# Gated linear attention and two expert layers on one core: ScalarE's order in the first two expert steps is taken from the program

## The chip, the core and the metric

The kernel runs on one core of a Trainium2 chip. The metric is the device time of one execution in microseconds (us), as the median of several runs. Beside it there is one profiled execution, from which the trace comes. TensorE is PE in the profile (its weight loads are PEld), VectorE is DVE, ScalarE is ACT, GpSimd is POOL and SyncE, which issues most transfers, is SP.

## The reference, cut to what matters

```python
state = f[t, :, None] * state + outer(k[t], v[t])        # f = sigmoid(f_logit), per head
y[t]  = q[t] @ state                                     # 4 x 8 heads, 768 tokens, width 48
x     = y laid out as (3072 tokens, 384)
x     = square(relu(x @ w_in)) @ w_out                   # 384 -> 2048 -> 384
logits = x @ w_gate                                      # 8 experts
e      = argmax(logits, axis=1)                          # one expert for each token
out[n] = softmax(logits)[n, e[n]] * (relu(x[n] @ w1[e[n]]) @ w2[e[n]])   # 384 -> 1024 -> 384
```

All of it is float32. Products that need full precision are made of three matmuls: each operand is split into a rounded part (`hi`) and the rest (`lo`), and the sum takes lo with hi, hi with lo and hi with hi.

## The kernel before

The first part walks through eight groups of 384 tokens. For each group it makes the attention output, then the first expert layer in 16 slices i (`moe_h` gives `ph`, `moe_act` gives `gg`, `gh` and `gl`, `moe_out` adds into `po`), and then the routing of its tokens (`route`). TensorE, ScalarE, VectorE and GpSimd run in the written order there. `moe_out` of a slice is issued two slices after its `moe_h`, so the last two slices of the last group have their `moe_out` back to back at its end.

The second part has expert steps. A step of kind D takes 256 tokens of one expert through that expert's two matrices in 8 slices: `step_h` (9 matmuls into `ph`, then `hh` on ScalarE and `hl` on VectorE) and, two slices later, `step_out` (6 matmuls into `qo`). The weights of one step come in eight pieces j (`load_w`, SyncE's queue, 384 KB each) into `raw`; each piece is then split (`split_w`, `split_part`): ScalarE makes `w_hi`, and VectorE or GpSimd makes `w_lo` (for step 1, GpSimd has the odd j, by `lo_pool`). A piece of `raw` can be loaded again when both have read it. Two sets of `w_hi` and `w_lo` alternate: step 0 and step 2 use set 0, step 1 uses set 1, which held the second matrix of the first layer until the last group's `moe_out`.

Step 0's pieces are split in the last group. Step 1's pieces are issued in the program's text in step 0, by `split_plan`, in the order j = 0, 1, 4, 2, 5, 3, 6, 7, each behind one slice's `step_h`. Also in step 0, `final_tables` runs piecewise through `hook`: it finishes the routing of the last group (`route`: logits `pl`, the one-hot `oh`, the counts `pc`, the rows `abr`, the table `pslot`) and computes which expert and which tokens the steps from 2 on take (down to `esi` for the weights and `sel`, `pi`, `ids` for the tokens). This is a chain of some eighty small VectorE instructions with four stops on TensorE (`pl`, `pc`, `pslot`, `pi`), whose places among TensorE's matmuls are fixed.

What sets the order: a scheduler in the compiler orders the instructions of each engine by its own estimate of when they can run, and may move them far from their place in the text. For engines named in `manual_schedule` the order is the program's. In the first two steps this is TensorE only, in the later ones TensorE and ScalarE. VectorE, GpSimd and SyncE are ordered by the scheduler in all steps.

Of the kernel before, what the change touches and what calls it, by code (L numbers as in the profile page):

```python
# [56 lines left out]
def gla_moe_moe_kernel(ctx: ExitStack, tc: tile.TileContext, qk, ft, vt, w_in, w_out, w_gate, w_gateT, w_e, q, k, v, f_logit, out, dbg=None):  # L57
# [969 lines left out]
    def run_steps(s0, s1, hook=None, pend=(), flush=True):  # L1027
        pend = list(pend)
        for s in range(s0, s1):
            if s == NALWAYS - 1:  # L1030
                tc.mark_branch_hint_location("rest")
            for i in range(8):
                pend.append((s, i, *step_h(s, i)))
                while len(pend) > (2 if KINDS[s] == "D" else 3):
                    step_out(*pend.pop(0))
                if i == 0 and s + 2 != NEARLY:
                    load_x(s + 2)
                if KINDS[s] == "S" and i % 2:
                    load_w(s + 1, i // 2)
                for t, j in SPLITS.get((s, i), ()):  # L1040
                    split_w(t, j)
                    if t + 1 != NEARLY or early["ready"]:
                        load_w(t + 1, j)
                if hook:
                    hook(s, i)
                if i == (5 if KINDS[s] == "D" else 3):
                    prep_next(s + 1)
        if flush:
            for p in pend:
                step_out(*p)  # L1050
        return pend
# [3 lines left out]
        if s < NEARLY:  # L1055
            next(fin, None)

    with tc.manual_schedule(engines={mybir.EngineType.PE}):
        left = run_steps(0, NEARLY, hook, flush=False)
    with tc.manual_schedule(engines={mybir.EngineType.PE, mybir.EngineType.Activation}):  # L1060
        run_steps(NEARLY, NALWAYS, pend=left)
# [291 lines left out]
```

## Time and profile before

| | |
|---|---|
| median of 3 runs | 834.55 us (834.1 to 838.1) |
| the profiled execution's own time | 835.33 us |
| its span, first to last instruction | 833.6 us |
| TensorE busy | 797.7 us, 96% of the span |
| VectorE busy | 554.3 us, 66% |
| ScalarE busy | 412.6 us, 49% |
| GpSimd busy | 160.0 us, 19% |
| granted TensorE clock, mean | 0.99 |

The span lies 1.7 us below the own time, and the own time 0.8 us above the median. In the trace the last group runs from 496.6 to 558.5 us, step 0 from 558.5 to 579.8, step 1 to 598.8.

### The profile page before, as it was taken

How to read it: one execution, taken by the hardware profiler on the slowest of the kernel's cores; microseconds unless marked ns; L12 is line 12 of the kernel's file. 1: busy time of each engine (PE TensorE's matmuls, PEld its weight loads, DVE VectorE, ACT ScalarE, POOL GpSimd, SP SyncE). 2: the span in 40 equal slices, each digit the busy share in tenths (PEclk: the TensorE clock that was granted, in tenths of full speed). 3: DMA queues.
4: the chain of work that ended last, by engine and by line, in shares of the span. 5: the costliest groups of instructions: out<-in, count | busy, mean ns of one | idle time of the engine just before them, and what ended most of it. 6: DMA issues, size and time to landing. Idle time of an engine off the chain costs nothing.

```text
span 833.6 us, 14582 instructions
## 1 busy us (share of the span) xinstructions
PE 797.7 (96%) x5343; PEld 747.8 (90%) x5343; DVE 554.3 (66%) x1266; ACT 412.6 (49%) x814; POOL 160.0 (19%) x154
## 2 busy tenths in 40 slices
PE   5799999999999999999999999989999899999995
PEld 4566669999999999999999999989999899898995
DVE  7988769867767757857757844558467555556641
ACT  2233366454455455455454454662565565556551
POOL 2000000000000000000000002021666556555651
PEclk9999999999999999999999999999999999999998
DMA  9786410121130121131130015322866676868640
GB/s 245 215 247 200 128 38 22 41 76 41 40 95 22 41 76 41 40 84 34 40 77 1 1 37 190 105 77 83 292 214 194 229 256 204 270 194 270 194 150 28
DMA packets 40687, 100.61 MB, mean 121 GB/s; under 512 B 5662, under 2 KB 12642, under 8 KB 40480
## 3 DMA queue, kind: packets, MB, share of 16 engines
q1 hardware_dynamic: 37024, 90.14, 36.0%
q0 software_dynamic: 3584, 9.46, 3.0%
q8 instruction: 44, 0.72, 0.4%
q14 instruction: 35, 0.29, 0.1%
HBM read 89.73 MB, written 10.24 MB: 120 GB/s over the span
## 4 chain that ended last, share of the span: by engine, by line
PE 76%; DVE 7%; DMA 6%; issue 5%; ACT 4%; POOL 0%; SPq 0%; POOLq 0%; DVEq 0%; ACTq 0%
PE po L421 21%; PE ph L391 20%; PE qo L984 8%; PE ph L964 8%; DVE w_lo L596 4%; DMA raw<-w_e 4%; PE pa L271 3%; PE py L310 3%; PE ph L381 3%; PE py L301 2%; ACT w_hi L595 2%; PE pu L295 2%; PE ph L952 2%; DMA xT<-xT 2%; PE pk L264 1%
## 5 line engine op out<-in xcount | busy, mean ns | idle before, releaser
L397 ACT ACTIVATE gg<-ph 128x384 f32<-128x384 f32 x128 | 62.7, 490 | 177.2 <-PE ph L391 121.8
L404 DVE TENSOR_TENSOR gl<-gg,gh 128x384 fp32r<-128x384 f32 x112 | 63.4, 566 | 92.8 <-ACT gh L402 91.5
L391 PE MATMUL ph<-xh,w_lo 128*128 128x384 f32 x336 | 119.0, 354 | 1.0 <-ACT gg L397 1.0
L421 PE MATMUL po<-w_hi,gl 128*128 128x384 f32 x336 | 113.5, 338 | 2.3 <-DVE gl L404 2.3
L391 PE MATMUL ph<-xl,w_hi 128*128 128x384 f32 x336 | 114.8, 342 | 0.6 <-DVE xl L168 0.6
L391 PE MATMUL ph<-xh,w_hi 128*128 128x384 f32 x336 | 114.3, 340 | 0.0
L421 PE MATMUL po<-w_hi,gh 128*128 128x384 f32 x336 | 113.3, 337 | 0.0
L421 PE MATMUL po<-w_lo,gh 128*128 128x384 f32 x336 | 112.9, 336 | 0.0
L596 DVE TENSOR_TENSOR w_lo<-raw,w_hi 128x768 fp32r<-128x768 f32 x63 | 94.3, 1499 | 24.9 <-ACT w_hi L595 19.8
L596 POOL TENSOR_TENSOR w_lo<-raw,w_hi 128x768 fp32r<-128x768 f32 x49 | 90.7, 1868 | 83.7 <-ACT w_hi L595 81.4
L595 ACT ACTIVATE w_hi<-raw 128x768 fp32r<-128x768 f32 x112 | 93.8, 839 | 21.8 <-DMA raw<-w_e 20.5
L969 DVE SCALAR_TENSOR_TENSOR hl<-ph,hh 128x256 fp32r<-128x256 f32 (+1 forms) x128 | 48.8, 386 | 77.7 <-ACT hh L968 73.5
L691 POOL MEMSET xg<- 128x385 f32 x4 | 2.1, 556 | 479.3 <-PE py L301 479.3
L968 ACT ACTIVATE hh<-ph 128x256 fp32r<-128x256 f32 (+1 forms) x128 | 45.2, 356 | 96.0 <-PE ph L964 75.7
L964 PE MATMUL ph<-xh,w_lo 128*128 128x256 f32 x288 | 82.7, 287 | 5.9 <-DVE w_lo L596 5.9
L445 DVE SCALAR_TENSOR_TENSOR junk<-rows,wgb 128x384 f32<-128x384 f32 x144 | 79.8, 554 | 3.3
L964 PE MATMUL ph<-xl,w_hi 128*128 128x256 f32 x288 | 81.2, 282 | 0.0
L964 PE MATMUL ph<-xh,w_hi 128*128 128x256 f32 x288 | 81.0, 281 | 0.0
L391 PEld LDWEIGHTS ph<-xh,w_lo 128*128 128x128 f32 x336 | 63.1, 188 | 7.3 <-issue 3.3
L398 ACT ACTIVATE gg<-gg 128x384 f32<-128x384 f32 x128 | 67.2, 525 | 4.0
L984 PE MATMUL qo<-w_hi,hl 128*128 128x384 f32 x192 | 66.4, 346 | 1.9 <-DVE hl L969 1.2
L421 PEld LDWEIGHTS po<-w_hi,gl 128*128 128x128 f32 x336 | 63.1, 188 | 2.9 <-DVE gl L404 2.7
(226 smaller groups left out, 1682.0 us busy)
## 6 DMA issues: line engine op xcount, KB each, us to landing
raw<-w_e SPq DMA_DIRECT2D x128, 384.0 KB
qk<-qk SPq DMA_DIRECT2D x46, 192.0 KB
stg<-w_in SPq DMA_DIRECT2D x8, 768.0 KB
stg<-w_out SPq DMA_DIRECT2D x8, 768.0 KB
f<-ft SPq DMA_DIRECT2D x24, 226.2 KB
xs<-rows SPq DMA_DIRECT2D x8, 577.5 KB
v<-vt SPq DMA_DIRECT2D x24, 192.0 KB
wgb<-w_gateT SPq DMA_DIRECT2D x1, 1536.0 KB
```

What stands on the lines that cost most here:

```text
L391: nc.tensor.matmul(ph, lhsT=w[:, sl], rhs=x[:, k, :], start=(n == 0), stop=(n == 8))
L397: nc.scalar.activation(out=gg, in_=ph, func=AF.Relu)
L398: nc.scalar.activation(out=gg, in_=gg, func=AF.Square)
L404: nc.vector.tensor_tensor(out=gl, in0=gg, in1=gh.bitcast(F32), op=ALU.subtract)
L421: nc.tensor.matmul(po[m], lhsT=a[:, sl], rhs=w[:, ws], start=(i == 0 and n == 0), stop=(i == NF - 1 and n == len(terms) - 1),)
L445: nc.vector.scalar_tensor_tensor(out=junk, in0=rows[:, m, 0:DM], scalar=1.0, in1=wgb[0][:, e, :], op0=ALU.mult, op1=ALU.mult, accum_out=lg ...
L595: nc.scalar.activation(out=hi, in_=src, func=AF.Copy)
L596: eng.tensor_tensor(out=lo, in0=src, in1=hi.bitcast(F32), op=ALU.subtract)
L964: nc.tensor.matmul(ph, lhsT=wslice(s, w, (i * 3 + k) * 128, 128), rhs=x[:, k, :], start=(n == 0), stop=(n == 8))
L968: nc.scalar.activation(out=hh, in_=ph, func=AF.Relu)
L969: nc.vector.scalar_tensor_tensor(out=hl, in0=ph, scalar=0.0, in1=hh.bitcast(F32), op0=ALU.max, op1=ALU.subtract)
L984: nc.tensor.matmul(out_t[s][m], lhsT=x[:, sl], rhs=wslice(s, w, 3 * F2 + i * DM, DM), start=(i == 0 and n == 0), stop=(i == 7 and n == 2),)
```

## The change

ScalarE is added to the engines whose order is the program's in steps 0 and 1.

```diff
-    with tc.manual_schedule(engines={mybir.EngineType.PE}):
+    with tc.manual_schedule(engines={mybir.EngineType.PE, mybir.EngineType.Activation}):
         left = run_steps(0, NEARLY, hook, flush=False)
```

No instruction is added or taken away; TensorE's order is the same. ScalarE's order changes, and with it the scheduler's orders for VectorE, GpSimd and SyncE. In the rows below `raw_5027` to `raw_5034` are the pieces j = 0 to 7, `w_hi_150` is set 0 and `w_hi_151` set 1, and `hh<-ph_5698`, `5730`, `5767`, `5820`, `5842` belong to the slices 0 to 4 of step 0.

ScalarE at the end of the last group and the start of step 0, before: the last three instructions of the last group's last slice (L397, L398, L402) stand behind a split of step 1's piece 5.

```order
L595 ACTIVATE w_hi_151<-raw_5032 128x768
L397 ACTIVATE gg<-ph 128x384
L398 ACTIVATE gg<-gg 128x384
L402 ACTIVATE gh<-gg 128x384
L595 ACTIVATE w_hi_150<-raw_5033 128x768
L595 ACTIVATE w_hi_150<-raw_5034 128x768
L438 ACTIVATE rows<-po_5171 128x384
L438 ACTIVATE rows<-po_5173 128x384
L595 ACTIVATE w_hi_151<-raw_5033 128x768
L968 ACTIVATE hh<-ph_5698 128x256
```

The same place in the changed kernel:

```order
L397 ACTIVATE gg<-ph 128x384
L398 ACTIVATE gg<-gg 128x384
L402 ACTIVATE gh<-gg 128x384
L595 ACTIVATE w_hi_150<-raw_5033 128x768
L595 ACTIVATE w_hi_150<-raw_5034 128x768
L438 ACTIVATE rows<-po_5171 128x384
L438 ACTIVATE rows<-po_5173 128x384
L968 ACTIVATE hh<-ph_5698 128x256
L595 ACTIVATE w_hi_151<-raw_5027 128x768
L463 ACTIVATE xt_5044<-pt 128x384
L968 ACTIVATE hh<-ph_5730 128x256
L595 ACTIVATE w_hi_151<-raw_5028 128x768
```

All eight splits of step 1, six of which stood in the last group, now stand in step 0, one behind each `hh`. Step 2's first six splits (`w_hi_150` of the pieces 0, 1, 4, 2, 5, 3), which stood between the second and the fourth `hh` of step 1, stand one behind each `hh` from step 1's third on.

VectorE between `oh` and the counts `pc` in step 0 (a piece of the difference; `sl` is the first instruction that reads `pc`, and om, ex and ss belong to the gate's value, which is off the way to `pslot`):

```order
 L479 SCALAR_TENSOR_TENSOR rk<-d,rev 128x24
 L481 TENSOR_REDUCE rm<-rk 128x3
-L535 TENSOR_SCALAR om<-ex 128x24
 L483 TENSOR_TENSOR oh<-rev,rm 128x24
-L536 RECIPROCAL om<-om 128x24
 L969 SCALAR_TENSOR_TENSOR hl<-ph_5767,hh 128x256
-L537 TENSOR_TENSOR ex<-ex,om 128x24
-L539 TENSOR_REDUCE ss<-ex 128x3
+L596 TENSOR_TENSOR w_lo<-raw_5031,w_hi_151 128x768
 L496 TENSOR_TENSOR sl<-pc,base 128x24
-L540 TENSOR_SCALAR ss<-ss 128x3
 L497 TENSOR_TENSOR base<-pc,base 128x8
```

A split of piece 4 now stands ahead of `sl`. A little further on, up to the rows `abr` from which `pslot` is made:

```order
+L596 TENSOR_TENSOR w_lo<-raw_5029,w_hi_151 128x768
 L639 TENSOR_REDUCE nb_5892<-gt_5890 128x8
 L504 TENSOR_SCALAR hl<-si 128x3
 L505 TENSOR_SCALAR hl<-si 128x3
-L969 SCALAR_TENSOR_TENSOR hl<-ph_5820,hh 128x256
+L969 SCALAR_TENSOR_TENSOR hl<-ph_5842,hh 128x256
 L825 TENSOR_TENSOR nb_5886<-nb_5886,nb_5892 128x8
 L507 CAST hf<-hl 128x6
 L826 TENSOR_TENSOR nb_5892<-nb_5892,taken 128x8
-L830 SCALAR_TENSOR_TENSOR co<-one_5052,nb_5886 128x8
+L535 TENSOR_SCALAR om<-ex 128x24
 L515 TENSOR_SCALAR abr_5046<-iblk,hf,tok_85 128x96
```

A split of piece 2 and the `hl` of slice 4 now stand ahead of `abr`, and so does `om`, which waits for ScalarE's `ex`. Further on a split of piece 6 stands between `pslot` and `sel`. On GpSimd the splits of the pieces 1, 5 and 3, three of which stood in the last group, now stand behind the tables' constants, ahead of that of piece 7 and of the gathers of step 2's tokens. On SyncE the loads of step 2 keep their places; those of step 3 now stand behind the reads of all later steps' expert numbers and of `tot`.

## Rows read from the trace of the kernel before

**Rows 1.** The waits of TensorE over the span: total us, times, longest us.
```profile
PE ph L964 <- DVE w_lo L596: 5.9, 3, 2.0
```
**Rows 2.** The chain that ended last, in order of time: start us, us, what.
```profile
505.60 1.57 PE po L421 x9
...
550.06 3.24 DMA raw<-w_e
...
562.00 1.06 PE ph L964 x9
```
**Rows 3.** The timeline of ScalarE at the last group's end: start us, us, idle before.
```profile
553.33 0.85 ACT L595 ACTIVATE w_hi<-raw 128x768 fp32r<-128x768 f32 x1 [2.04 <-DMA raw<-w_e]
554.08 0.47 ACT L397 ACTIVATE gg<-ph 128x384 f32<-128x384 f32 x1
```
**Rows 4.** The timeline of TensorE: earlier in the last group, and at its end.
```profile
507.01 1.14 PE L460 MATMUL pt<-ident,rows 128*128 128x128 f32 x9
507.91 0.42 PE L391 MATMUL ph<-xh,w_lo 128*128 128x384 f32 x1
...
553.87 0.34 PE L421 MATMUL po<-w_hi,gh 128*128 128x384 f32 x1
556.54 0.44 PE L421 MATMUL po<-w_hi,gl 128*128 128x384 f32 x1 [2.33 <-DVE gl L404]
...
561.75 0.36 PE L964 MATMUL ph<-xh,w_lo 128*128 128x256 f32 x1
```
**Rows 5.** Windows: stretch, length, busy us of PE, PEld, DVE, ACT, POOL; PEclk; DMA.
```profile
559.50:560.50 1.00, 1.00 (x7) 1.00 (x6) 0.00 (x0) 0.00 (x0) 0.00 (x0) 0.50 0.70 194
...
666.00:667.00 1.00, 1.00 (x10) 1.00 (x10) 0.59 (x1) 0.47 (x2) 0.00 (x0) 1.00 0.73 252
```
**Rows 6.** The timeline of TensorE in step 0: the stops of the tables.
```profile
567.03 0.18 PE L488 MATMUL pc<-oh,tri 128*128 128x8 bf16 x1
...
571.60 0.52 PE L530 MATMUL pslot<-abr 128*96 128x256 f32 x3
...
579.55 0.39 PE L655 MATMUL pi<-sel,slot 96*128 96x18 f32 x2 [0.39 <-DVE sel L651]
```
**Rows 7.** The timeline of VectorE in step 0.
```profile
567.45 0.18 DVE L496 TENSOR_TENSOR sl<-pc,base 128x24 f32<-128x24 f32 x1
...
570.79 0.32 DVE L515 TENSOR_SCALAR abr<-iblk,hf,tok 128x96 fp32r<-128x96 bf16 x1
571.03 0.35 DVE L523 TENSOR_SCALAR abr<-ipos,hf 128x256 fp32r<-128x256 bf16 x1
...
579.32 0.17 DVE L651 TENSOR_TENSOR sel<-wso,pp 96x18 fp32r<-96x18 f32 x1
```
**Rows 8.** A window over most of step 0.
```profile
562.00:580.00 18.00, 17.61 (x138) 17.08 (x138) 15.36 (x85) 4.84 (x12) 1.81 (x1) 1.00 0.10 35
```
**Rows 9.** The timeline of TensorE in step 1: first matmuls of four slices.
```profile
584.21 0.28 PE L964 MATMUL ph<-xh,w_lo 128*128 128x256 f32 x1
...
587.60 0.28 PE L964 MATMUL ph<-xh,w_lo 128*128 128x256 f32 x1
...
589.73 0.28 PE L964 MATMUL ph<-xh,w_lo 128*128 128x256 f32 x1
...
591.83 0.28 PE L964 MATMUL ph<-xh,w_lo 128*128 128x256 f32 x1
```
**Rows 10.** The timelines of VectorE and GpSimd where both split.
```profile
601.24 0.96 DVE L596 TENSOR_TENSOR w_lo<-raw,w_hi 128x768 fp32r<-128x768 f32 x1 [0.31 <-ACT w_hi L595]
...
605.60 4.82 DVE L596 TENSOR_TENSOR w_lo<-raw,w_hi 128x768 fp32r<-128x768 f32 x1 [0.31 <-ACT w_hi L595]
...
605.93 3.66 POOL L596 TENSOR_TENSOR w_lo<-raw,w_hi 128x768 fp32r<-128x768 f32 x2
...
533.29 1.85 POOL L596 TENSOR_TENSOR w_lo<-raw,w_hi 128x768 fp32r<-128x768 f32 x1 [22.66 <-ACT w_hi L595]
...
534.21 1.34 DVE L404 TENSOR_TENSOR gl<-gg,gh 128x384 fp32r<-128x384 f32 x1 [3.09 <-ACT gh L402]
```

## The prediction, made before the changed kernel ran

> **What bounds the kernel now.** I read the waits of TensorE first, then the chain that ended last, and then the timelines of the four engines around the places where it leaves TensorE. TensorE is busy for 96% of the span, so what counts is where it stands still. Between 505 and 600 us the chain goes off to the loads of `raw`: step 1's piece landing at 553.3 us ends a load of 3.24 us [rows 2]. ScalarE had waited 2.04 us for it, because a split of step 1's piece 5 stands in its order ahead of the last slice's `gg`, and `gg` starts only at 554.08 [rows 3]. TensorE's last `moe_out` needs `gl` and starts at 556.54, where the `po` before it began at 553.87: with the usual 0.17 between two starts 2.5 us are lost [rows 4]. Then the granted clock falls: it is 0.50 at 560 us, the lower of its two levels, 1.2 in place of 2.4 GHz [rows 5]. From 556.54 to the second `ph` of step 0 at 561.75 it takes 5.2 us; at full clock 9 `po` take 1.57, 9 `ph` 1.06 [rows 2] and the 9 transposes 0.90 (507.01 to 507.91) [rows 4], in all 3.53. So the fall cost 1.7. Three other waits of 2.0 us [rows 1] brought no fall (the clock is 1.00 behind the one that ended at 665.5 [rows 5]).
>
> Step 0 is bound otherwise. VectorE is busy 15.36 of the 18 us from 562 to 580, ScalarE 4.84 and GpSimd 1.81 [rows 8]: the tables keep VectorE nearly full. The last `abr` ends at 571.38 and TensorE takes `pslot` at 571.60 without a wait; for `pi` it waits 0.39 us for `sel` [rows 6, 7]. In step 1 a slice takes 2.10 us (589.73 to 591.83), but the one at 584.21 takes 3.39: 1.3 us are lost [rows 9], where ScalarE has step 2's splits ahead of the copies that free `qo`.
>
> **The change part by part.**
>
> *What it removes.* In the last group ScalarE waits for no piece of step 1 any more; step 0's pieces had landed before (their splits start without a wait for a transfer). `gg` of the last slice follows its `ph` as in the other slices, `gl` is ready by 553.4, and TensorE goes on at 554.04. That removes 2.5 of wait and 1.7 of clock. Everything in step 0 now lies 4.2 us earlier. The 1.3 of step 1 goes as well: two `hh` and both `qo` copies stand ahead of step 2's splits. The wait of 0.4 at `pi` is counted anew below, so it comes off too. Removed in all: 2.5 + 1.7 + 1.3 + 0.4 = 5.9 us.
>
> *What ScalarE takes up in step 0.* Eight splits of 0.85 [rows 3], 6.8 us, beside 4.84 of work in 18 [rows 8]. Each stands behind an `hh` and can hold up the next one by at most 0.85; `step_out` uses `hh` and `hl` two slices later, more than 2 us on. Cost nothing. If that cover were gone it would be up to 0.85 a slice.
>
> *What VectorE takes up.* Four splits, 0.96 each when VectorE is alone [rows 10], in an engine that is full. I walk the new order row by row with the durations of the trace, TensorE 4.2 us earlier (`pc` 562.9 in place of 567.03).
> First stop, `pslot`. `hh` of slice 2 ends at 562.4, ScalarE's split of piece 4 at 563.15, VectorE's at 564.1. Only then comes `sl`, for which `pc` was there at 563.3: 0.8 late. The split of piece 2 costs 0.9 a little later. `hl` of slice 4 must now pass ahead, and `om` waits 0.3 for `ex`, which on ScalarE stands behind the split of piece 5 and ends at 567.8. The six `abr` end at 569.55. TensorE has done its matmuls at 567.44 (571.60 less 4.16). It waits 2.1 us. In short: about 2.3 more on the way from `pc` to `abr`, less the 0.2 that this way had to spare [rows 6, 7].
> Second stop, `pi`. The way from `pslot` to `sel` gets the split of piece 6 (0.9) and the gate's small instructions, which were earlier before; the old wait of 0.4 becomes 1.4 if nothing else happens.
>
> *GpSimd beside VectorE.* This is the cost that the trace shows only for large instructions. At 605.60 VectorE starts a split and takes 4.82 us in place of 0.96; GpSimd works on two splits from 605.93 to 609.59 [rows 10]. VectorE stands still while GpSimd splits, though it had begun first. A `gl` of 384 elements takes 1.34 with GpSimd's split ending at 535.14 [rows 10]. Both read two tensors from SBUF, as many of the tables' instructions do. In the changed step 0 GpSimd splits four pieces, 1.85 each [rows 10], where it split one. Piece 1 falls beside the argmax, where TensorE has two slices of other work; piece 5 beside the six `abr`, which read one tensor and by the rows of other such instructions go on; piece 3 (572.4 to 574.25) beside the tables behind `pslot`, and piece 7 (577.3 to 579.2) beside VectorE's own split of piece 6, which starts at 576.9. The bounds are nothing, as for an instruction with one SBUF operand, and all of what is left of 1.85 at each collision. The nearest rows are held wholly, so I take that: 3.3 more at `pi`, 4.7 us in all.
>
> The Trainium skill (SBUF — State Buffer, section Who interferes with whom) says that a VectorE instruction with two SBUF inputs contends with a GpSimd instruction that reads SBUF, which the rows bear out. It also says that whichever issues first has the ports for the whole instruction; the row at 605.60 says otherwise, since VectorE was first by 0.33 us and lost. By the page the split of piece 6 would keep going; that is a rival below.
>
> *The clock.* A wait of 2.5 was followed by the fall, three of 2.0 were not. The wait at `pslot`, 2.1, lies between; that at `pi`, 4.7, lies above. I take one fall, 1.7; bounds none and two.
>
> *What moves at no cost.* Step 2's gathers of tokens start about 2 us later, but are read at 594; its loads keep their places in SyncE's queue and come 2 us later than before, while the first split that needs one moved back by more. The transfer of the last group's rows is issued some 4 us later and still ahead of those gathers. Step 3's loads, pushed behind the reads on SyncE, are split a step later, past 600 us. From there on the order is the old one and the whole tail only shifts.
>
> **Sum.** Added 2.1 + 4.7 + 1.7 = 8.5, removed 5.9: plus 2.6 us. On the profiled execution's own 835.33 that is 837.9; the median lies 0.8 below that execution, so the forecast is 837.1, 0.3% above 834.55. This is within 0.5% (4.2 us), about what a measurement of this kernel can tell from no change.
>
> **The rivals.**
>
> *Small instructions aren't held.* Then `pi` costs 1.4: 2.1 + 1.4 - 5.9 = -2.4 us, 832.2; with a fall of the clock after `pslot` -0.7, 833.8. For it: the tables' instructions are far shorter than those held in the rows, and no row has one beside a split. Against it: nothing in the held ones depends on their length. Chance 0.2.
>
> *Who starts first keeps the ports.* The split of piece 6 starts 0.4 ahead of GpSimd's piece 7 and isn't held, so `pi` costs 2.9: 2.1 + 2.9 + 1.7 - 5.9 = +0.8, 835.4. Against it speaks the 4.82. This is the rule of the Trainium skill's page SBUF — State Buffer. Chance 0.15.
>
> *Slower: `abr` is held too.* The six `abr` read one tensor, but the one with 256 columns takes 0.35 and the one with 96 takes 0.32 [rows 7]: 160 columns more for 0.03 us, where a split of 768 takes 0.96. So it runs in a faster way, and may need more ports. Held from 568.2 to 569.6 beside piece 5, `pslot` waits 3.6 and the clock falls there as well; `pi` then still waits 3.1 and may bring a second fall: 3.6 + 3.1 + 3.4 - 5.9 = +4.2, 838.8; with `pi` at 4.7 as above +5.8, 840.4. It decides from about 1 us of holding at `abr`. The Trainium skill (same page, same section) says that tensor_scalar can enter a mode that contends. Chance 0.18.
>
> **How the numbers follow.** The forecast's own case has 0.45, with 835.2 (no fall of the clock) to 838.5 (two). The remaining 0.02 is for what I don't see. The range goes from the first rival's 832.0 to 839.6, inside the third. Faster by over 0.5% (below 830.4) is reached by no case that I worked out: 0.04. Slower by over 0.5% (above 838.7) is most of the third rival and the end of the forecast's: 0.18. Within: 0.78.
>
> **What would show it.** Right: TensorE has no wait at the last `moe_out` and the clock is 1.00 there; a wait of about 2 at `pslot` for `abr`, and a longer one at `pi` for `sel`; VectorE rows with two SBUF inputs stretched beside GpSimd's splits of the pieces 3 and 7; no loss in step 1's third slice. Wrong: a wait for `hl` in step 0, a wait of ScalarE for step 2's pieces in step 1, or a later shift of more than 1 us behind 600 us.

## The result, and the profile after

The changed kernel takes 840.77 us (median of 7 runs, 840.43 to 842.35); the kernel before takes 834.95 beside it (7 runs). The recorded ratio is 1.0057, 95% interval 1.0042 to 1.0073: slower by a little over half a per cent. It is not the quotient of the two medians, which is 1.0070: of the seven times before, four lie at 834.1 to 835.0 and three at 837.5 to 838.1, so its median is lower than its mean of 835.94. So the change costs 4.8 us by the ratio and 5.8 by the medians; the median lies 3.7 us above the forecast. The profiled execution took 840.74 us, its span is 838.9, and the mean granted clock is 0.982 in place of 0.990.

The waits of TensorE after the change (total us, times, longest us), where [rows 1] showed the three of 2.0:

```profile
PE ph L964 <- DVE w_lo L596: 6.4, 4, 2.0
PE pi L655 <- DVE sel L651: 3.5, 2, 3.1
PE pslot L530 <- DVE abr L523: 2.7, 1, 2.7
```

The wait of 2.3 for `gl` [rows 4] is gone. Two waits have come, for `abr` and for `sel`. The chain that ended last (start us, us, what) now leaves TensorE in other places than in [rows 2]:

```profile
550.21 4.72 PE po L421 x27
554.93 1.06 PE ph L964 x9
...
566.97 1.77 DVE om L535
568.74 0.24 DVE abr L515
...
570.29 0.53 PE pslot L530
570.82 1.94 PE ph L964 x9
572.84 0.39 ACT hh L968
573.26 0.43 DVE hl L969
574.11 1.80 DVE io L870
...
578.03 0.86 DVE w_lo L596
...
579.75 1.35 DVE eso L879
582.15 0.39 PE pi L655 x2
...
583.72 1.86 PE qo L984 x6
585.61 1.89 PE ph L964 x9
587.50 1.05 PE qo L984 x6
```

The reader is to see three things. The last group ends in one stretch of 27 `po` without a gap. In step 0 the chain goes over three small VectorE instructions of 1.35 to 1.80 us: `om` (128 x 24 elements), `io` (128 x 8) and `eso` (128 x 18). And twice, behind `pslot` and behind `pi`, nine `ph` take 1.9 us in place of 1.06: the clock has fallen. The windows say so (stretch, length, busy us of PE, PEld, DVE, ACT, POOL; PEclk; DMA share, GB/s), beside the one fall of [rows 5], which is gone:

```profile
571.00:572.00 1.00, 1.00 (x7) 1.00 (x6) 1.00 (x9) 0.00 (x0) 0.00 (x0) 0.50 0.00 0
...
586.00:587.00 1.00, 1.00 (x7) 1.00 (x6) 0.16 (x1) 0.00 (x0) 0.70 (x2) 0.50 0.95 353
669.00:670.00 1.00, 1.00 (x7) 1.00 (x6) 0.26 (x1) 0.66 (x1) 0.00 (x0) 0.50 0.77 218
```

The third of these lies behind one of the old waits for `w_lo`. TensorE's timeline has the marks between which the next sections count (start us, us; `px` is the first transpose of a step's tokens, in the last group and then in step 1; the numbers ahead of them answer to [rows 6]):

```profile
544.63 0.82 PE L624 MATMUL px<-ident,xg 128*128 128x128 f32 x6
...
569.38 1.44 PE L530 MATMUL pslot<-abr 128*96 128x256 f32 x3 [2.66 <-DVE abr L523]
...
582.15 0.39 PE L655 MATMUL pi<-sel,slot 96*128 96x18 f32 x2 [3.07 <-DVE sel L651]
...
597.03 0.82 PE L624 MATMUL px<-ident,xg 128*128 128x128 f32 x6
```

Why the small instructions are long is seen where VectorE's timeline is laid beside GpSimd's, the same stretch of both, as in [rows 7, 10]. GpSimd's four splits of step 1:

```profile
559.28 1.82 POOL L596 TENSOR_TENSOR w_lo<-raw,w_hi 128x768 fp32r<-128x768 f32 x1 [48.23 <-ACT w_hi L595]
566.90 1.80 POOL L596 TENSOR_TENSOR w_lo<-raw,w_hi 128x768 fp32r<-128x768 f32 x1 [5.81 <-ACT w_hi L595]
574.04 1.84 POOL L596 TENSOR_TENSOR w_lo<-raw,w_hi 128x768 fp32r<-128x768 f32 x1 [5.33 <-ACT w_hi L595]
579.26 1.80 POOL L596 TENSOR_TENSOR w_lo<-raw,w_hi 128x768 fp32r<-128x768 f32 x1 [3.39 <-ACT w_hi L595]
```

And VectorE beside them:

```profile
560.20 0.18 DVE L475 TENSOR_REDUCE mx<-lg 128x3 f32<-128x24 f32 x1
560.42 0.72 DVE L477 TENSOR_TENSOR d<-lg,mx 128x24 f32<-128x24 f32 x1
...
566.97 1.77 DVE L535 TENSOR_SCALAR om<-ex 128x24 f32<-128x24 f32 x1
568.65 0.32 DVE L515 TENSOR_SCALAR abr<-iblk,hf,tok 128x96 fp32r<-128x96 bf16 x1
...
569.89 0.34 DVE L523 TENSOR_SCALAR abr<-ipos,hf 128x256 fp32r<-128x256 bf16 x1
...
574.02 1.88 DVE L870 TENSOR_SCALAR io<-io,over 128x8 f32<-128x8 f32 x1
...
577.95 0.95 DVE L596 TENSOR_TENSOR w_lo<-raw,w_hi 128x768 fp32r<-128x768 f32 x1
...
579.67 1.43 DVE L879 TENSOR_TENSOR eso<-eso,odd 128x18 f32<-128x18 f32 x1
```

Each of GpSimd's splits has one VectorE instruction that ends with it: 559.28 + 1.82 is 561.10, and `d` ends at 561.14; 568.70 against 568.74; 575.88 against 575.90; 581.06 against 581.10. `d` and `eso` read two tensors. `om` and `io` are of the form tensor_scalar and read one (`io` beside it a single value for each partition). `mx`, a reduction in the middle of the first split, went on. The row at 569.89 is the last of the six `abr`; it ends at 570.23.

### The profile page after: what moved, and what is told of

The parts are those of the page before. It is cut to its first block, busy times and chain, and to the rows that moved or that the text cites. A ratio compares the mean times of both kernels' runs of the same rounds, so it can differ in the third digit from the quotient of the medians.

```text
span 838.9 us, 14587 instructions
## 1 busy us (share of the span) xinstructions
PE 799.3 (95%) x5343; PEld 748.8 (89%) x5343; DVE 555.9 (66%) x1266; ACT 412.7 (49%) x814; POOL 159.8 (19%) x154
## 4 chain that ended last, share of the span: by engine, by line
PE 79%; DVE 8%; issue 5%; DMA 4%; ACT 2%; POOL 0%; SPq 0%; POOLq 0%; DVEq 0%; ACTq 0%
PE po L421 23%; PE ph L391 22%; PE qo L984 8%; PE ph L964 8%; DVE w_lo L596 4%; PE pa L271 3%; PE py L310 3%; PE ph L381 3%; PE py L301 2%; PE pu L295 2%; DMA raw<-w_e 2%; DMA xT<-xT 1%; PE pk L264 1%; ACT w_hi L595 1%; PE ph L952 1%
## 5 line engine op out<-in xcount | busy, mean ns | idle before, releaser
L397 ACT ACTIVATE gg<-ph 128x384 f32<-128x384 f32 x128 | 62.8, 491 | 185.9 <-PE ph L391 129.0
L596 DVE TENSOR_TENSOR w_lo<-raw,w_hi 128x768 fp32r<-128x768 f32 x63 | 92.3, 1466 | 18.9 <-ACT w_hi L595 14.2
L398 ACT ACTIVATE gg<-gg 128x384 f32<-128x384 f32 x128 | 67.3, 526 | 4.1
L984 PE MATMUL qo<-w_hi,hh 128*128 128x384 f32 x192 | 65.4, 341 | 0.0
```

The lines of the kernel that those rows point to most:

```text
L397: nc.scalar.activation(out=gg, in_=ph, func=AF.Relu)
L398: nc.scalar.activation(out=gg, in_=gg, func=AF.Square)
L596: eng.tensor_tensor(out=lo, in0=src, in1=hi.bitcast(F32), op=ALU.subtract)
L984: nc.tensor.matmul(out_t[s][m], lhsT=x[:, sl], rhs=wslice(s, w, 3 * F2 + i * DM, DM), start=(i == 0 and n == 0), stop=(i == 7 and n == 2),)
```

## The experiments

Twelve kernels ran, in three groups, each beside runs of the kernel before on the same chip (832.24, 836.33 and 835.38 us in median), so ratios are compared, and stretches of the trace. The ratios are the recorded estimates and can differ from the quotient of the medians (for e12 0.9937 and 0.9960). The stretches come from one execution each. "Steps 0 and 1" below is the time from `px` in the last group to `px` in step 1: 48.47 us before (593.95 less 545.48), 52.40 after (597.03 less 544.63). The waits are those of TensorE ahead of these instructions in the profiled execution, and "falls" counts the falls of the clock between the two marks.

| kernel | ratio to before (95%) | steps 0 and 1 | at `pslot` | at `pi` | falls |
|---|---|---|---|---|---|
| before | 1 | 48.47 | 0 | 0.39 | 1 |
| after | 1.0057 (1.0042 to 1.0073) | 52.40 | 2.66 | 3.07 | 2 |
| e4_after_again | 1.0044 (1.0029 to 1.0059) | 54.54 | 2.66 | 2.79 | 2 |
| e8_step1_alone | 1.0003 (0.9986 to 1.0021) | 48.56 | 0 | 0.39 | 1 |
| e9_step0_alone | 1.0089 (1.0054 to 1.0124) | 56.48 | 2.66 | 3.83 | 3 |
| e6_no_gpsimd_lo | 0.9968 (0.9958 to 0.9978) | 46.09 | 1.07 | 1.21 | 0 |
| e7_no_vector_lo | 1.0004 (0.9983 to 1.0025) | 49.13 | 0 | 4.68 | 1 |
| e3_no_lo | 0.9958 (0.9936 to 0.9979) | 43.56 | 0 | 0.96 | 0 |
| e1_all_on_vector | 1.0016 (0.9998 to 1.0035) | 52.59 | 1.90 | 2.82 | 2 |
| e2_all_on_gpsimd | 1.0052 (1.0032 to 1.0072) | 53.41 | 2.93 | 4.43 | 2 |
| e10_om_on_scalar | 1.0025 (1.0008 to 1.0043) | 51.98 | 2.45 | 2.94 | 1 |
| e11_pi_a_slice_later | 1.0005 (0.9987 to 1.0023) | 48.89 | 2.66 | 1.19 | 1 |
| e5_early_and_late | 0.9961 (0.9938 to 0.9985) | 43.56 | 0 | 0.96 | 0 |
| e12_early_late_pi | 0.9937 (0.9919 to 0.9955) | 42.33 | 0 | 0 | 0 |

Theory A is the prediction's own: in step 0 the splits of step 1 make VectorE late, partly by VectorE's own four, more by GpSimd's four, which hold VectorE up; rival B: the loss is mainly VectorE's own load, whoever stands beside it; rival C: it lies in step 1 or later.

**The changed kernel once more (e4_after_again), no edit.**

> The changed kernel once more, beside the same runs of the kernel before as the next three. If the loss lies in steps 0 and 1 (theory: a wait of 2.7 at pslot, one of 3.1 at pi, two falls of the clock of 1.7, less what was removed): the start of the third step lies 3 to 4 us further behind the last group than before, the ratio is 1.004 to 1.006, and the waits at pslot and pi are within 0.3 of 2.7 and 3.1. If the shifts of 1.5 and 0.7 us in the later steps are a consequence of the order, they come again and TensorE waits over 5 us in all for w_lo there; if they belong to that one execution or that chip, TensorE waits under 3 us for w_lo and nothing more is lost behind step 2.

840.09 against 836.33 us. The waits at `pslot` and `pi` came again; the falls lasted longer in this execution (the windows from 570 to 576 and from 584 to 590 are at 0.50), which makes steps 0 and 1 longer by 2.1, so they lie 6.1 us above before and not the 3 to 4 that were expected. The wait for `w_lo` was 5.9 in all, as before, so the 6.4 of the first trace belongs to that execution; since before has the same 5.9, this wait doesn't tell what the order does to the later steps.

**Step 1 alone and step 0 alone (e8, e9).**

```diff
-    with tc.manual_schedule(engines={mybir.EngineType.PE, mybir.EngineType.Activation}):
-        left = run_steps(0, NEARLY, hook, flush=False)
+    with tc.manual_schedule(engines={mybir.EngineType.PE}):
+        left = run_steps(0, 1, hook, flush=False)
+        with tc.manual_schedule(engines={mybir.EngineType.Activation}):
+            left = run_steps(1, NEARLY, hook, pend=left, flush=False)
```

This is e8; e9 has the inner line around step 0 in place of step 1.

> ScalarE's order is the program's in step 1 only; the last group and step 0 keep the scheduler's order with the wait of 2.3 at the last moe_out. My sum: step 1 gives back its 1.3 in the third slice and nothing else changes, so the ratio is 0.998 to 0.9995 (minus 1.3 us), no wait at pslot, 0.4 at pi. Rival, that the splits of step 2 set the pace in step 1 in any order: third slice on time, but the loss is found again in step 2 as a wait for w_lo, ratio 1.000.

> ScalarE's order is the program's in step 0 only; in step 1 the scheduler places step 2's splits ahead of the copies of qo, as before. If the parts add up (my sum): the loss of the changed kernel plus the 1.3 of step 1, so 1 to 1.5 us slower than the changed kernel, ratio to before 1.005 to 1.008, and waits at pslot and pi as in the changed kernel (2.7 and 3.1). Rival, that the waits of step 0 give step 1's splits and copies time and hide the loss there: no slower than the changed kernel.

Both missed. In e8 the third slice of step 1 came on time and its `step_out` waited instead:

```profile
590.00 0.44 PE L984 MATMUL qo<-w_hi,hl 128*128 128x384 f32 x1 [1.26 <-DVE hl L969]
```

The `hh` ahead of that `hl` started at 589.10 on ScalarE after 4.41 us of idleness, though the nine matmuls of its `ph` had run from 583.30 to 584.51; no row shows what it waited for, and this stays open. The changed kernel and e10 have such a gap too, of 3.67 and 3.71 us, ahead of the same `hh`, and in each of the three one transfer on the queue that the profile calls "q14 instruction" falls into it (in the microsecond from 586 in e8, 590 in after, 588 in e10). That `hh` waited for this transfer is not shown. In e9 the loss of step 1 was larger than the 1.3 of before: TensorE waited 2.12 at 592.00 for ScalarE's copy of `qo`, and the clock was 0.68 from 592 to 595. So the order in step 1 is worth nothing behind the old step 0 and 56.48 - 52.40 = 4.1 us behind the new one in these executions (3.8 by the ratios of e9 and e4, whose intervals overlap). Rival C falls: the loss against before comes with step 0's order.

**Without GpSimd's four splits, without VectorE's four, without all eight (e6, e7, e3).** For e6; e7 has `j % 2 == 0`, e3 has no condition on j:

```diff
+        if s == 1 and j % 2:
+            nc.scalar.activation(out=wst_[1][j][0], in_=rawt[j], func=AF.Copy)
+            return
         split_part(*wst_[s % 2][j], rawt[j], nc.gpsimd if j in lo_pool(s) else nc.vector)
```

> The changed kernel without GpSimd's four w_lo of step 1 (pieces 1, 3, 5, 7; only w_hi is made of them, so step 1 multiplies with what stood there). VectorE keeps its four. If GpSimd's splits hold up VectorE's rows (theory): om takes about 0.1 in place of 1.77, io about 0.1 in place of 1.88, eso 0.1 in place of 1.43; TensorE waits at pslot 0.9 to 1.3 in place of 2.7, at pi 1.0 to 2.0 in place of 3.1, the clock stays at 1.00 in step 0 and at the start of step 1, and the kernel is 4 to 7 us faster than the changed kernel (ratio to before 0.996 to 1.000). Rival, that VectorE's own four splits make the waits: pslot stays above 2.0, pi above 2.5, the gain on the changed kernel is under 2 us.

> The changed kernel without VectorE's four w_lo of step 1 (pieces 0, 2, 4, 6; only w_hi is made of them, so step 1 multiplies with what stood there). GpSimd keeps its four. Theory, that one split on VectorE costs it 0.86 to 0.95 and one beside it on GpSimd 1.3 to 1.7: VectorE gets back some 3.5 us, three of the four splits ahead of pslot and pi and one behind; TensorE waits 0 to 0.9 at pslot and 2 to 3 at pi, at most one fall of the clock, 2 to 5 us faster than the changed kernel, and less is won than without GpSimd's four (6.3 us). Rival, that VectorE's own splits are the larger part: over 6 us faster than the changed kernel and no wait over 1.2.

> The changed kernel without step 1's eight w_lo subtractions (left out; the old contents stand in for them). ScalarE's order and its eight splits in step 0 stay. If the loss is VectorE's way through the tables, made longer by its own four splits and held by GpSimd's four, both waits shrink to at most 0.4 us, the clock stays at 1.00 through steps 0 and 1 and the time falls to about 830 us, below before. If ScalarE's order itself costs (ex late, hh behind splits), the wait at pslot stays near 2 us and the time above 837.

Without GpSimd's four, steps 0 and 1 take 46.09 in place of 52.40, 6.3 us less, as much as the median fell (833.82 against 840.09 in the same group). VectorE in e6, the instructions that were held:

```profile
566.59 0.18 DVE L535 TENSOR_SCALAR om<-ex 128x24 f32<-128x24 f32 x1
566.68 0.33 DVE L515 TENSOR_SCALAR abr<-iblk,hf,tok 128x96 fp32r<-128x96 bf16 x1
...
567.93 0.35 DVE L523 TENSOR_SCALAR abr<-ipos,hf 128x256 fp32r<-128x256 bf16 x1
...
571.36 0.23 DVE L870 TENSOR_SCALAR io<-io,over 128x8 f32<-128x8 f32 x1
...
575.64 0.17 DVE L879 TENSOR_TENSOR eso<-eso,odd 128x18 f32<-128x18 f32 x1
```

The same instructions, in the same order on VectorE, take 0.18, 0.23 and 0.17 in place of 1.77, 1.88 and 1.43, and in steps 0 and 1 no wait is left that the clock falls behind. Without VectorE's own four, 3.3 us are won (52.40 - 49.13; by the ratios 0.40%, also 3.3). There the whole lateness stands at `pi`, one wait of 4.68 where 2 to 3 was expected, and VectorE's trace has three instructions of 1.44 to 1.80 beside GpSimd's splits in it. So A holds and B does not: GpSimd's four cost more than VectorE's four, whose 3.3 us are part of the loss all the same. Without all eight (e3) what is left is 43.56: this is the changed kernel without any of its new losses, with a wait of 0.96 at `pi` (at most 0.4 was expected) that the tables alone leave.

**All eight on VectorE, all eight on GpSimd (e1, e2).**

```diff
     def lo_pool(s):
+        if s == 1:
+            return ()
         return (3, 5, 7) if KINDS[s - 1] == "S" else (1, 3, 5, 7)
```

e2 has `tuple(range(8))`.

> The changed kernel with all eight w_lo of step 1 on VectorE, none on GpSimd. If GpSimd's splits are what holds om, io and eso, these take 0.2 us each again, VectorE pays 3.5 us more of its own, and the two waits together fall from 5.7 to about 4.5: some 838 to 840 us. If the holding has another cause, om and io stay near 1.8 us and the time rises above 842.

> The changed kernel with all eight w_lo of step 1 on GpSimd. VectorE loses four splits (3.8 us) and GpSimd gets four more (7.4 us). If VectorE's own splits are the larger part of the loss, the waits shrink to under 3 us together and the time to about 837. If GpSimd's holding is, the waits grow above 6 us together and the time to 842 or more.

Taking the splits from VectorE makes it later, not earlier: 2.93 and 4.43 of waits with none on VectorE, 1.90 and 2.82 with all, where `om`, `io` and `eso` took 0.17, 0.20 and 0.17 again. The ratios go the same way, 1.0052 and 1.0016, with intervals that just touch; both are lower than was expected of these kernels. A split on VectorE itself takes 0.86 of the chain; three of GpSimd's four in the changed kernel take 1.3 to 1.7 from it, and that of piece 1 holds `d` for 0.5 where it costs nothing. GpSimd in e2 has splits at 562.58 (1.85) and 565.02 (1.84), and VectorE beside them:

```profile
562.65 0.18 DVE L496 TENSOR_TENSOR sl<-pc,base 128x24 f32<-128x24 f32 x1 [0.31 <-PE pc L488]
562.87 0.17 DVE L497 TENSOR_TENSOR base<-pc,base 128x8 f32<-128x8 f32 x1
562.95 1.52 DVE L498 TENSOR_TENSOR sl<-sl,oh 128x24 f32<-128x24 f32 x1
...
565.13 0.40 DVE L639 TENSOR_REDUCE nb<-gt 128x8 f32<-128x96 f32 x2
565.46 1.43 DVE L504 TENSOR_SCALAR hl<-si 128x3 uint32<-128x3 uint32 x1
```

The two that read `pc` from PSUM and one tensor from SBUF go on, as do two reductions; `sl<-sl,oh` with two tensors in SBUF is held, and so is a tensor_scalar on three integers. The Trainium skill (SBUF — State Buffer, section Who interferes with whom) says that two SBUF inputs contend with GpSimd's reads, that tensor_scalar can, and that tensor_reduce never does on this chip. The rows agree on all three.

**`abr` beside GpSimd's split (e10).** In the changed kernel `om` took the hold and `abr` came when it was over. Here `om` of the last group is made on ScalarE, and `abr` stands in its place.

```diff
+        if g == NG - 1:
+            nc.scalar.activation(out=om, in_=ex, func=AF.Copy, scale=-1.0, bias=1.0)
+        else:
-        nc.vector.tensor_scalar(out=om, in0=ex, scalar1=-1.0, scalar2=1.0, op0=ALU.mult, op1=ALU.add)
+            nc.vector.tensor_scalar(out=om, in0=ex, scalar1=-1.0, scalar2=1.0, op0=ALU.mult, op1=ALU.add)
```

> The changed kernel with the last group's om made on ScalarE behind ex, so that the six abr stand where om stood on VectorE, beside GpSimd's split of piece 5. If abr is held like om (my rival of the prediction: tensor_scalar needs the ports): the first or second abr takes 1.5 to 1.9 in place of 0.32, pslot waits 2.4 to 2.7 as before and the time is that of the changed kernel (ratio to before 1.003 to 1.006). If abr goes on (what the sum assumed): six rows of 0.32 to 0.35, pslot waits 0.9 to 1.3, and the time is 1 to 3 us below that of the changed kernel. If whoever starts first keeps going, the first abr, begun 0.1 us before GpSimd's split, takes 0.32 and the second is held.

VectorE; GpSimd's split of piece 5 ran from 566.09 to 567.89:

```profile
565.95 0.17 DVE L833 TENSOR_TENSOR_SCAN co<-one,nb 128x8 f32<-128x8 f32 x1
566.03 1.93 DVE L515 TENSOR_SCALAR abr<-iblk,hf,tok 128x96 fp32r<-128x96 bf16 x1
567.88 0.34 DVE L523 TENSOR_SCALAR abr<-ipos,hf 128x256 fp32r<-128x256 bf16 x1
```

`abr` is held, 1.93 in place of 0.32, and `pslot` still waits 2.45, as the first alternative said; the ratio is a little under its 1.003 to 1.006. Its row begins 0.06 ahead of GpSimd's, but the one ahead of it ends only at 566.12, so the run doesn't decide who was first. The ratio is 0.19% below that of e4, with intervals that overlap. The wait of 2.94 at `pi` was followed by no fall (a clock of 1.00 from 581 to 586); the stretch from `pi` to `px` took 14.71 even so, with two waits, of 0.46 at 587.97 and 0.61 at 592.53, that the changed kernel does not have.

**`pi` a slice later (e11).**

```diff
+        yield
         pi = yield from lookup(T, go, n, "1")
...
-                if i == 0 and s + 2 != NEARLY:
+                if i == (s == 1) and s + 2 != NEARLY:
```

> The changed kernel with pi one slice (2.1 us) later in TensorE's order, and with it the gathers of step 2's and step 3's tokens. VectorE's work isn't changed. If the loss at pi is lateness against a fixed place: the wait there is 0.7 to 1.3 in place of 2.8 to 3.1, the second fall of the clock (1.7) is gone, and the kernel is 3 to 4 us faster than the changed kernel (ratio to before 0.999 to 1.001). Rival: the gathers come late, TensorE waits over 1 us for xg at the start of step 2's transposes, and under 1 us is won.

As the first alternative said: wait 1.19, no second fall, 3.5 us less in steps 0 and 1, and a ratio 0.39% below that of e4. The lateness of `sel` is a loss only against TensorE's fixed place for `pi`.

**Splitting what has landed early, the rest late (e5, e12).** The pieces 0 to 4 of step 1 are split in the last group, in the program's order and late enough to have landed, and 5 to 7 in step 1, behind its first slices; step 0 keeps none. e12 has e11's edit as well.

```diff
+                for j in {8: [0], 11: [1], 13: [2], 14: [3], 15: [4]}.get(i, ()):
+                    split_part(*wst_[1][j], rawt[j], nc.gpsimd if j in (1, 3) else nc.vector)
...
-    early["split"], early["ready"] = [], False
+    early["split"], early["ready"] = [0, 1, 2, 3, 4], False
...
+    for key in list(SPLITS):
+        SPLITS[key] = [(u, j) for u, j in SPLITS[key] if u != 1]
+    for i, j in ((0, 5), (1, 6), (2, 7)):
+        SPLITS[1, i] = [(1, j)] + SPLITS.get((1, i), [])
```

> The changed kernel with the splits of step 1's pieces 0 to 4 written into the last group, each behind a slice by which its piece has landed, and those of 5, 6 and 7 into step 1. Step 0 has no split. If the two reasons are the whole of it (ScalarE waiting for a piece before; VectorE's tables after), neither the wait of 2.5 us at the last group's end nor the ones at pslot and pi appear, the clock stays, and the time is 829 to 830 us, 0.6% below before. If something else in the new order costs, it stays above 833.

> The kernel that splits the pieces 0 to 4 of step 1 in the last group and 5 to 7 in step 1 (e5_early_and_late), with pi one slice later as well. Theory: its wait of 1.0 at pi goes, nothing else changes in steps 0 and 1, 5.5 to 7 us faster than before in the steps 0 and 1 (from the last group's transposes to the first of step 2's), ratio to before 0.991 to 0.995. Rival: the later gathers are missed in step 2 and the ratio is 0.995 to 0.998, no better than without.

e5 has in steps 0 and 1 the 43.56 of the kernel without these splits: put there, they cost nothing in these steps. Its time is 0.4% below before, not the 0.6% that was expected. e12 takes 42.33, 6.1 below before, and 832.08 against 835.38 us: the lowest ratio of all, 0.6% below the kernel before (0.4% by the medians, from four runs). The intervals of e5 and e12 overlap, so that e12 is the better of the two is not shown. Its profiled execution has a fall of the clock at 660 to 670 us (mean 0.83) that the trace of before does not have.

## Why the prediction was wrong, step by step

The marks of the trace give each term of the sum. A base without new losses is e3 and e5: from `px` to `pslot` 21.92, from `pslot` to `pi` 7.53 (8.49 less the wait of 0.96), from `pi` to `px` 13.14.

- **Removed, 5.9 predicted: right.** Before, the three stretches are 26.12, 7.95 and 14.40: 4.2 + 0.4 + 1.3 = 5.9 above the base. After the change, the last group has no gap, and the slice of step 1 that took 3.39 [rows 9] takes 2.10 (588.39 to 590.49).
- **`pslot`, 2.1 predicted: 3.5 by the same count.** The forecast counted from the moment when TensorE is free to the end of the last `abr`. In the changed kernel these are 566.72 (569.38 less 2.66) and 570.23. (The wait of 2.66 in the trace ends earlier, since the first of `pslot`'s three matmuls needs two of the six `abr` only.) The step that failed is "piece 5 beside the six `abr`, which read one tensor and by the rows of other such instructions go on". GpSimd's piece 5 held `om`, which stands ahead of `abr`, for 1.6 us (1.77 less 0.18), a cost that the sum put at nothing, and e10 shows `abr` held as well. VectorE's own part, forecast as these 2.1, was nearly right: without GpSimd's four, in e6, the same count gives 1.9 (566.35 to 568.28).
- **`pi`, 4.7 predicted: 4.6.** TensorE reaches `pi` 37.52 after `px`, where the base without waits takes 29.45; of these 8.07, 3.51 are counted at `pslot`. The collisions at the pieces 3 and 7, predicted as 3.3, took 1.65 at `io` and 1.26 at `eso`, 2.9 in all; `io` is a tensor_scalar on one tensor and again not of the kind that the sum counted, so the size of this term is in part luck. The rest, predicted as 1.4, is 1.7. VectorE's split of piece 6 ran at 577.95 in 0.95, ahead of GpSimd's piece 7 and beside nothing, so the rival on who starts first was not put to the test there.
- **The clock, one fall of 1.7 predicted: two falls.** The first, behind `pslot`, is covered by the lateness of `sel`: TensorE would have waited longer at `pi` without it. The second, behind `pi`, costs 14.88 - 13.14 = 1.74; e11, without it, needs 11.01 from `pi` to `px`, the base less a slice of 2.1. So the term was right in size for steps 0 and 1, by the wrong count. e10 has no second fall and needs 14.71 all the same, 1.57 above the base, of which its two waits are 1.07; so without the fall other waits can take its place.
- **Sum for steps 0 and 1, +2.6 predicted: +3.9** (8.07 + 1.74 - 5.88). The 1.3 between them is the hold at `pslot`, since the other terms came out within 0.2.
- **"From there on the order is the old one and the whole tail only shifts": wrong for the profiled execution.** Behind the wait for `w_lo` that ends at 668.52 the clock fell, and 1.5 us are lost there (the next `px` lies at 682.32 against 677.73, 4.6 later, after 3.1 at 597.03). The same wait, 1.96 to 1.98 long, was followed by no fall in before [rows 5], in e7 and in e9, and by one in after, e4, e6, e8, e10, e11 and e12. The rest is 0.7 behind 730 us, of it 0.5 in a fourth wait for `w_lo` at 769.89 that e4 does not have. Against these stand 0.85 by which the changed kernel was already ahead at the last group, where nothing was changed.
- **From the execution to the median.** I took the median 0.8 below the profiled execution, as it was for the three runs of before; for the changed kernel the two agree (840.77 and 840.74). With 1.3 from steps 0 and 1, 1.5 + 0.7 behind them, 0.1 outside the span, less 0.85, this makes up the 3.7 us within 0.1. So the step that failed explains about a third of the miss, and the rest of it is not shown to come from the change.
- **The bounds.** The forecast's own case without a fall and with two is 835.4 and 838.8 by its own terms (0.9 and 4.3 above 834.55), not 835.2 and 838.5.

By mechanism, the rival that came true is the one forecast as slower, which gave 838.8 to 840.4: a tensor_scalar in front of `pslot` is held, so that `pslot` is 3.6 late by its sum and 3.5 in the trace, the clock falls there, and again behind `pi`. I gave it 0.18, because other rows of one-input instructions had gone on. Those that stand inside GpSimd's splits in the trace of before read PSUM (`hl`, and `lg` at 565.00) or copied one value for each partition (`gate`), a difference that I did not look for.

The rival "who starts first keeps the ports" got 0.15 because of the row at 605.60, where I took VectorE to be first. That reading overlooked what GpSimd did ahead of its two splits, and another place of the same trace. GpSimd, then VectorE and GpSimd at the other place:

```profile
604.91 1.00 POOL L997 DMA_INDIRECT out<-o,ids  x1 [0.30 <-ACT hh L968]
...
542.34 0.96 DVE L596 TENSOR_TENSOR w_lo<-raw,w_hi 128x768 fp32r<-128x768 f32 x1 [0.18 <-ACT w_hi L595]
...
543.12 1.90 POOL L596 TENSOR_TENSOR w_lo<-raw,w_hi 128x768 fp32r<-128x768 f32 x1 [7.98 <-ACT w_hi L595]
```

At 605.60 GpSimd had been at work since 604.91 and went over to its splits at 605.93. At 542.34 GpSimd was idle, VectorE began its split 0.78 ahead of GpSimd's and kept its 0.96. The held rows in steps 0 and 1 of the changed kernel began behind GpSimd's split, but for `io`, whose row begins 0.02 ahead of it while the instruction ahead of it still runs. So these rows do not speak against that rival's rule, and no run here was made to test it.

What stays open is the clock. In these traces the waits of 1.90 and more in steps 0 and 1 were followed by a fall in all cases but the 2.94 of e10, those up to 1.26 in none; the first wait of 2.0 further on went either way, the two behind it brought no fall. The length of the wait alone does not decide it, and no run here separates what does. So the 1.5 us behind 668 us are not shown to come from the change.

## What to carry to other kernels

When work goes to GpSimd to relieve a full VectorE, count what it holds there: here a split on GpSimd cost VectorE's chain 1.3 to 1.7 us in three of four cases, the split on VectorE itself 0.86. Sort VectorE's instructions by operation and by where their operands lie before saying which are held: a tensor_scalar of 24 elements stood still for a whole split, a reduction beside it did not. And when an order by hand removes a wait, look at which engine the moved work lands on in the next stage: of the places tried, the best for these splits was neither the scheduler's nor the program's, but the one in which the transfer had landed and no table was under way.

## What the runs showed of the hardware

- Held instructions of up to 96 elements for each partition end within 0.07 us of GpSimd's split, whatever their size: 3 elements (1.43, e2), 8 (1.88, after), 24 (1.77, after), 96 of bf16 (1.93, e10). One of 144 elements, which takes 0.30 alone in e6, ended 0.17 behind it (e2, 577.62). GpSimd's own splits beside these take 1.80 to 1.85.
- A fall of the clock can cost nothing: from `pslot` to `pi` TensorE spent 2.17 us more on its work than the base (0.74 in e6, where the clock did not fall), and the wait at `pi` was that much shorter.
- ScalarE stood 3.67 us (after) and 4.41 us (e8) ahead of the `hh` of step 1's third slice with its `ph` done, without a visible reason; behind it TensorE lost 0.2 and 1.26 us.
